# Plain float32 products for the first batch, and float16 weight parts made once behind it

## The chip, the cores and the metric

The kernel runs on one core of one Trainium2 chip. The time is device microseconds of one execution. TensorE (PE in the profile; PEld is its weight load) does the matrix products, VectorE (DVE) and ScalarE (ACT) the elementwise work, GpSimd (POOL) very little, and SyncE (SP) issues the DMAs.

## The reference

Attention over 8 batches, 8 heads, 576 positions, 64 columns a head, and then a gated layer over the 512 columns of all heads:

```python
scores = where(0 <= i - j < 128, q @ k.T / 8 - slope[h] * |i - j|, -1e9)
x = softmax(scores) @ v                      # heads side by side: 576 x 512
h = maximum(x @ w_in, 0)                     # w_in 512 x 1024
u, v = h[:, :512], h[:, 512:]
v_n = (v - mean(v)) / sqrt(var(v) + 1e-6)    # over its 512 columns
v_s = w_spatial @ v_n + b_spatial[:, None]   # w_spatial 576 x 576
out = (u * v_s) @ w_out                      # w_out 512 x 512
```

The weights `w_in` and `w_out` come as 64-bit floats, all else as float32.

## The kernel before

A batch has four pairs of heads and one gated stage. A pair's two heads stand on the two halves of the partitions. For batches 1 to 7 a pair takes: load (`L`), the score products (`P`, line 791, plain float32 on 64x64 quarters of the array), softmax on VectorE and ScalarE (`C`, lines 805 to 851), a DMA that turns the probabilities, the split of the values (`V`) and the product with them (`A`, line 937), whose result is a tile of x, `xt`. Batch 0 does the same in small tiles of 128 positions, so that work starts early: `t` (line 686), `m`, `n` (lines 728 and 743).

The gated stage has units, each an accumulation in one PSUM bank of the two named `m`:

- `v`, five of them: 128 positions by 512 columns of x @ w_in (line 1026; the last, of 64 positions, lines 1048 and 1054), then relu, layer norm, and the split of v_n into two float16 parts;
- `u`, eight: 128 columns by 288 positions (line 1083), then relu;
- `s`, eight: the product over positions with w_spatial in float16 parts (line 1104), then the gate (line 1112) and a split of the gated tile `gs` (lines 413 and 1118);
- `o`, eight: the output product (line 1130), copied out and stored.

Every product of two float32 operands is made of three matmuls: high by high, high by low, low by high (`PASS`). Batches 0 and 1 take w_in and x as two parts of type float32r (one pass each); batches 2 to 7 (`HALVES = 2`) take float16 parts. The output product is in float32r parts in all batches. `split_w64` turns 64-bit weights into float32 with some bit operations on VectorE (lines 432 to 451) and then makes the two float32r parts: a rounding copy (line 413) and a difference (line 456). For batch 2, `H`, `J`, `K` find a power of two (`win_limit`, `win_scale`) and make float16 parts of w_in from the float32r parts (`win_halves`, lines 508, 515, 519). The values of batch 1 get a power of two each by an own chain with a DMA (lines 878 to 898), those of later batches one for each batch.

`Plan` sets the order. Each operation has an engine, a weight in ns and a due time. `record` adds operations in the order of the table `OPENING` (then of `usual`), which fixes what waits for what and which buffer each takes. `Plan.forward` then lets each engine take the ready operation with the smallest due time, and `backward` sets the due times anew; an operation that either of VectorE and ScalarE can do goes to the one free first. Each engine executes in the emitted order. Where the plan has TensorE idle for over 400 ns between 9 and 95 us, it puts in matmuls of ones that compute nothing (`filler`, line 339); 64 of the same kind stand at the start (line 396).

Of the kernel before, what the change touches and what calls it, by code (L numbers as in the profile page):

```python
# [209 lines left out]
def attn_gmlp_kernel(ctx, tc, qk, v, w_in, w_spT, b_sp, w_out, outT):  # L210
# [85 lines left out]
    win = {(h, c): plan.buf(work, f"win{h}{c}", 1, [P, 2, DH], F32R) for h in range(2) for c in range(NC_)}  # L296
    win16 = {}
    wend = fixed([P, 2, DH], F16, "wend")
    wlim = fixed([P, 2, NC_], F32, "wlim")
# [120 lines left out]
    def split_w64(src, dst, tmp, hi, lo, due):  # L420
# [46 lines left out]
    def win_weights(half, c, due, st):  # L467
        w = win[half, c]
        split_w64((st, DH), (w, ()), plan.buf(work, "gs", 5, [P, DH], F32), lambda: w()[:, 0, :], lambda: w()[:, 1, :], due)

    def power(out, least, low):
        nc.vector.tensor_reduce(least, wide()[:, 1, :], AX.X, ALU.max)
# [16 lines left out]
    def win_limit(half, c, due):  # L489
        if half and c == NC_ - 1:  # L490
            w = wend
        else:
            w = plan.buf(work, *(("vraw", 3) if half else (f"win1{c}", 1)), [P, 2, DH], F16)
        win16[half, c] = w

        def f():
            nc.scalar.activation(w()[:, 0, :].bitcast(BF16), win[half, c]()[:, 0, :].bitcast(F32), AF.Abs, accum_out=wlim()[:, half, c:c + 1])
        plan.add("ACT", act(DH, 2), due, f, [(win[half, c], (0,))], [(w, 0), (wlim, (half, c))])

    def win_scale(half, due):  # L500
        sc = lambda a, z: wsc()[:, half, a:z]
        spread(lambda: sc(2, 3), lambda: wlim()[:, half, :], due, [(wlim, (half, c)) for c in range(NC_)], [(wsc, (half, 2))])
        plan.add("DVE", 1025, due + 2, lambda: power(sc(0, 2), sc(3, 4), 2.0 ** -12), [(wide, 1), (pow2, 0)], [(wsc, half)])

    def win_halves(half, c, due):
        w, x, sc = win16[half, c], win[half, c], lambda: wsc()[:, half, 0:1]
        old = lambda k: x()[:, k, :].bitcast(F32)
        plan.either([("ACT", act(DH, 1), lambda: nc.scalar.activation(w()[:, 0, :], old(0), AF.Copy, scale=sc())),
                     ("DVE", dve(DH, True) + 50, lambda: nc.vector.tensor_scalar(w()[:, 0, :], old(0), sc(), None, ALU.mult))],
                    due, [(x, (0,)), (wsc, half)], [(w, 0)])  # L510

        t = plan.buf(work, "vt", 2, [P, DH], F32)

        def f():
            nc.vector.scalar_tensor_tensor(t(), old(0), sc(), w()[:, 0, :], ALU.mult, ALU.subtract)
        plan.add("DVE", dve(DH) + 50, due + 1, f, [(x, (0,)), (wsc, half), (w, 0)], [(t, 0)])

        def f():
            nc.vector.scalar_tensor_tensor(w()[:, 1, :], old(1), sc(), t(), ALU.mult, ALU.add)
        plan.add("DVE", dve(DH) + 50, due + 2, f, [(t, 0), (x, (1,)), (wsc, half)], [(w, 1)])  # L520
# [16 lines left out]
    def wsp_load(c, due):  # L537
# [6 lines left out]
        def f():  # L544
            nc.scalar.activation(wsp()[:, c, 1, :].bitcast(BF16), st(), AF.Abs, accum_out=rows()[:, c:c + 1])
        plan.add("ACT", act(S, 2), due, f, [(st, 0)], [(wsp, (c, 1)), (rows, c)])

    def rest_load(due):
# [10 lines left out]
        def f():  # L559
            nc.scalar.activation(r1().bitcast(BF16), rs(), AF.Abs, accum_out=rows()[:, NQ - 1:NQ])  # L560
        plan.add("ACT", act(S, 2), due, f, [(rs, 0)], [(r1, 0), (rows, NQ - 1)])

        def f():
            nc.scalar.activation(r2()[b1, :].bitcast(BF16), bt()[b1, :], AF.Abs, accum_out=rows()[b1, NQ:NQ + 1])
        plan.add("ACT", act(S, 2), due, f, [(bt, 0), (r2, 2), (rows, "z")], [(r2, 1), (rows, NQ)])

    def weights_scale(due):

        def f():
            nc.vector.tensor_reduce(rows()[:, LEAST:LEAST + 1], rows()[:, :NQ + 1], AX.X, ALU.max)  # L570
            nc.vector.tensor_copy(wide()[:, 0, :], rows()[:, LEAST:LEAST + 1].to_broadcast([P, P]))
        plan.add("DVE", 320, due, f, [(rows, c) for c in range(NQ + 1)], [(wide, 0)])

        def f():
            nc.sync.dma_start_transpose(out=wide()[:, 1, :], in_=wide()[:, 0, :])
# [9 lines left out]
        plan.add("DVE", 700, due + 2, f, [(wide, 1)], [(rows, "s")])  # L585
# [33 lines left out]
    def tail(xt, due):  # L619

        copy(R, lambda: (xt()[:, S:S + R], xt()[:, 2 * S:2 * S + R]), due, xcols(xt, 1, (NQ - 1) * P, S), [(xt, 2)], fast=True)

    def load(b, p, due, pieces, values, raw=None, vr=None):
# [3 lines left out]
        if values:  # L627
            vr = vr or plan.buf(work, "vraw", 3, [P, NQ, P], F32)
# [642 lines left out]
```

## Time and profile before

| what | us |
|---|---|
| median of 3 runs | 551.82 |
| lowest and highest of them | 549.66, 552.36 |
| the profiled execution | 549.37 |
| its span, from the first to the last instruction | 547.6 |
| TensorE matmul busy | 529.6 (97%) |
| VectorE, ScalarE busy | 449.8 (82%), 417.4 (76%) |

A share of the span is a mean over very different stretches. Matmul records overlap (the next begins before the one before has ended), so a busy TensorE may still do little; what a unit costs is read from one unit's start to the next's.

### The profile page before, as it was taken

Reading aid. Unit: us, or ns where it says so; the run is one execution under the profiler, and the core shown is the slowest. Engines: PE = TensorE matmul, PEld = TensorE weight load, DVE = VectorE, ACT = ScalarE, POOL = GpSimd, SP = SyncE. Lnnn points to the kernel's source line nnn. Section 1 sums busy time; section 2 is a strip of 40 time slices with the busy share of each in tenths; the row PEclk is TensorE's granted clock in tenths of the full one; section 3 lists DMA queues with packets and bytes.
Section 4 is the critical chain, followed back from the end, with each engine's and each line's share of the span. In section 5 each row is a group of like instructions: output and inputs, shape, how many; then the busy total and the mean of one; then the engine's idle time right before and its main releaser. Section 6 shows DMA issues by size and latency. Waiting matters only on the chain.

```text
span 547.6 us, 16355 instructions
## 1 busy us (share of the span) xinstructions
PE 529.6 (97%) x6240; PEld 420.9 (77%) x6240; DVE 449.8 (82%) x1685; ACT 417.4 (76%) x1331; POOL 30.4 (6%) x75
## 2 busy tenths in 40 slices
PE   8889998989999999999999999999999999999997
PEld 5546886878889668896789858896689858884787
DVE  6999999989999996979998889978998798525440
ACT  7999999989889686969898768766976777424322
POOL 0000010000100020000200010000100010001000
PEclk9999999999999999999999999999999999999999
DMA  7974563977486833697567775866186524410002
GB/s 227 381 262 147 123 171 84 210 130 173 70 188 156 233 67 91 140 238 191 115 137 176 184 137 86 178 160 118 45 125 168 98 60 68 89 47 22 1 1 88
DMA packets 128468, 73.75 MB, mean 135 GB/s; under 512 B 106755, under 2 KB 119043, under 8 KB 128389
## 3 DMA queue, kind: packets, MB, share of 16 engines
q1 hardware_dynamic: 128388, 72.70, 56.3%
q8 instruction: 49, 0.80, 0.6%
q14 instruction: 31, 0.25, 0.1%
HBM read 37.13 MB, written 9.44 MB: 85 GB/s over the span
## 4 chain that ended last, share of the span: by engine, by line
PE 74%; ACT 9%; DVE 9%; DMA 4%; issue 2%; SPq 1%; POOL 1%; POOLq 0%; ACTq 0%; DVEq 0%
PE m L1104 18%; PE m L1130 16%; PE m L1083 15%; PE m L1026 12%; PE s L791 6%; PE x L937 5%; DVE pq L845 2%; DMA vraw<-in_v_dram 2%; ACT prob L811 1%; DMA qkraw<-in_qk_dram 1%; PE m L1048 1%; DVE prob L805 1%; DMA vl<-vl 1%; ACT pq L840 1%; SPq L632 1%
## 5 line engine op out<-in xcount | busy, mean ns | idle before, releaser
L1104 PE MATMUL m<-wsp,vn 128*128 128x288 f16 x768 | 110.9, 286 | 0.5 <-DVE vn L1037 0.5
L811 ACT ACTIVATE prob<-prob,stat 128x192 f32<-128x192 f32 (+2 forms) x252 | 107.4, 432 | 1.6 <-DVE stat L805 1.3
L1083 PE MATMUL m<-xt,win 128*128 128x288 f16 (+1 forms) x768 | 102.9, 289 | 2.4 <-DVE u L1112 1.6
L1130 PE MATMUL m<-gs,wout 128*128 128x288 f32 x732 | 103.0, 298 | 2.1 <-ACT o L413 1.8
L1130 PEld LDWEIGHTS m<-gs,wout 128*128 128x128 f32 x732 | 98.0, 188 | 3.9 <-ACT o L413 2.0
L840 ACT ACTIVATE pq<-prob,stat 128x192 f16<-128x192 f32 (+2 forms) x252 | 89.9, 428 | 6.6 <-issue 3.4
L845 DVE SCALAR_TENSOR_TENSOR pq<-prob,stat,pq 128x192 f16<-128x192 f32 (+2 forms) x252 | 87.4, 389 | 2.1 <-ACT pq L840 1.9
L1104 PEld LDWEIGHTS <-vn 128*128 128x128 f16 x768 | 73.9, 98 | 19.9 <-DVE vn L1037 0.8
L805 DVE CUSTOM_DVE_ANT_0 prob<-s,tabs 128x192 f32<-128x192 f32 (+2 forms) x252 | 71.0, 329 | 4.5 <-PE s L791 4.4
L1083 PEld LDWEIGHTS <-win 128*128 128x128 f16 x576 | 55.8, 98 | 15.7 <-issue 0.4
L1026 PEld LDWEIGHTS <-xt 128*128 128x128 f16 x288 | 27.0, 98 | 33.1 <-issue 2.1
L1026 PE MATMUL m<-vraw,xt 128*128 128x512 f16 x216 | 50.7, 380 | 0.0
L811 ACT ACTIVATION_READ_ACCUMULATOR prob<-prob,stat 128x1 f32 x252 | 48.9, 194 | 0.0
L413 ACT CAST gs<-u 128x288 fp32r<-128x288 f32 x50 | 21.4, 429 | 36.0 <-DVE u L1112 35.8
L791 PE MATMUL s<-qkraw 64*64 64x192 f32 (+1 forms) x1008 | 43.5, 310 | 0.0
L937 PEld LDWEIGHTS <-vh 64*64 64x64 f16 x1232 | 34.8, 106 | 9.4 <-issue 6.6
L937 PE MATMUL x<-pt,vh 64*64 64x192 f16 (+2 forms) x1232 | 39.7, 224 | 1.7 <-POOL am L946 1.7
L1112 DVE SCALAR_TENSOR_TENSOR u<-m,vsc,u 128x288 f32<-128x288 f32 x48 | 24.7, 514 | 20.0 <-PE m L1104 19.5
L996 POOL TENSOR_TENSOR st<-st,nhalf 128x1 f32<-128x1 f32 (+1 forms) x40 | 26.4, 660 | 208.8 <-DVE st L992 196.2
L987 DVE BATCH_NORM_STATS2 st<-vt 128x6 f32<-128x512 f32 (+1 forms) x40 | 27.4, 687 | 12.6 <-ACT vt L417 12.6
L791 PEld LDWEIGHTS s<-qkraw 64*64 64x64 f32 x1008 | 36.5, 133 | 0.8 <-DVE stat L834 0.2
L1118 DVE TENSOR_TENSOR gs<-u,gs 128x288 fp32r<-128x288 f32 x61 | 27.2, 453 | 9.0 <-ACT gs L413 8.6
(203 smaller groups left out, 837.2 us busy)
## 6 DMA issues: line engine op xcount, KB each, us to landing
qkraw<-in_qk_dram SPq DMA_DIRECT2D x28, 576.0 KB, 4.7
out_dram<-o SPq DMA_DIRECT2D x64, 144.0 KB, 1.9
wraw<-in_v_dram SPq DMA_DIRECT2D x12, 320.0 KB, 3.2
win<-in_v_dram SPq DMA_DIRECT2D x12, 320.0 KB, 3.5
wout<-in_w_in_dram SPq DMA_DIRECT2D x4, 512.0 KB, 6.2
vn<-in_w_in_dram SPq DMA_DIRECT2D x4, 512.0 KB, 7.9
wout<-in_w_out_dram SPq DMA_DIRECT2D x4, 512.0 KB, 3.6
vraw<-in_v_dram SPq DMA_DIRECT2D x4, 320.0 KB, 4.4
```

What stands on the lines that cost most here:

```text
L791: nc.tensor.matmul(flat(bank)[rows, c0:c0 + n], raw()[j * D:(j + 1) * D, 0, i * D:(i + 1) * D], raw()[j * D:(j + 1) * D, 1, (i + 1) * D - ...
L805: nc.vector.tensor_tensor_reduce(pt(), flat(bank)[:, c0:c0 + n], tabs()[:, 2 * p + odd, W - n:], -0.125, 3e38, ALU.add, ALU.min, st()[:, N ...
L811: nc.scalar.activation(pt(), pt(), AF.Exp, bias=st()[:, NM, k:k + 1], scale=-1.0, accum_out=st()[:, SM, k:k + 1])
L840: nc.scalar.activation(pq()[:, qc:qc + n], prob()[:, pc:pc + n], AF.Copy, scale=st()[:, RC, k:k + 1])
L845: nc.vector.scalar_tensor_tensor(pq()[:, qc + PLANE:qc + PLANE + n], prob()[:, pc:pc + n], st()[:, RC, k:k + 1], pq()[:, qc:qc + n], ALU.m ...
L937: done.append(nc.tensor.matmul(xps[half]()[j * D:(j + 1) * D, x0:x0 + len(ks) * D], l()[rows, kb // 2, j * D:(j + 1) * D], ap, start=(half ...
L987: nc.vector.bn_stats(st()[:m, 0:6], vt()[:m])
L1026: nc.tensor.matmul(pt(), xs(xt[c], a, t * P, (t + 1) * P), w[1, c]()[:, k, :], start=(n == 0), stop=(n == 3 * NC_ - 1))
L1083: nc.tensor.matmul(pt()[:, :HS], w[0, c]()[:, k, d * P:(d + 1) * P], xs(xt[c], a, hf * HS, (hf + 1) * HS), start=(n == 0), stop=(n == 3 * ...
L1104: nc.tensor.matmul(pt()[:, :HS], l, r, start=(n == 0), stop=(n == len(ops) - 1))
L1118: nc.vector.tensor_tensor(gs()[:, 1, :], u(), gs()[:, 0, :].bitcast(F32), ALU.subtract)
L1130: nc.tensor.matmul(pt()[:, :HS], wout[d]()[:, w, e * P:(e + 1) * P], gs[d]()[:, a, :], start=(n == 0), stop=(n == 3 * ND - 1))
```

## The change

Batch 0 has x as one float32 tile and w_in and w_out as one float32 tile (`exact`, twelve buffers `wx`). Its `v`, `u` and `o` units take four plain float32 matmuls in place of twelve of one pass. Batches 1 to 7 all take float16 parts: `win_halves` makes those of w_in from the exact weights before batch 1, `wout_limit`, `wout_scale`, `wout_halves` (`h`, `q`, `Z`) three float16 tiles of w_out (high, low, high / 1024) before the `o` units of batch 1. The limits of w_in and w_spatial are summed by TensorE (a matmul of ones with absolute values, lines 500 and 584 to 586) and not by an accumulating ScalarE instruction and a DMA. Values of batch 1 are scaled like those of later batches. The float32r parts, the differences that made them, and the copy of x's tail go. `OPENING` is another permutation, with `h`, `q`, `Z`, and with `D`, `G`, `E`, `O` of batch 1 added. x tiles are kept by the pair's number.

```diff
-        copy(n, lambda: (hi(), x()), due + 4, [X], [HI], fast=True)
-
-        def f():
-            nc.vector.tensor_tensor(lo(), x(), hi().bitcast(F32), ALU.subtract)
-        plan.add("DVE", dve(n), due + 5, f, [X, HI], [LO])
...
     def win_weights(half, c, due, st):
+        x = exact[half, c] = plan.buf(work, "wx", WX, [P, DH], F32)
+        bits64((st, DH), x, due)
...
+                nc.tensor.matmul(pt(), sums()[:, 1, :], win[half, c]()[:, 0, :].bitcast(BF16), start=(c == 0), stop=(c == NC_ - 1))
+        plan.add("PE", pe16(*[DH] * NC_), due, f, [(win[half, c], 0) for c in range(NC_)] + [(sums, 0)], [(pt, 0)])
...
+    def parted16(w, x, sc, n, due, reads):
+        plan.either([("ACT", act(n, 1), lambda: nc.scalar.activation(w()[:, 0, :], x(), AF.Copy, scale=sc())),
+                     ("DVE", dve(n, True) + 50, lambda: nc.vector.tensor_scalar(w()[:, 0, :], x(), sc(), None, ALU.mult))],
+                    due, reads, [(w, 0)])
+
+        def f():
+            nc.vector.scalar_tensor_tensor(w()[:, 1, :], x(), sc(), w()[:, 0, :], ALU.mult, ALU.subtract)
+        plan.add("DVE", dve(n) + 50, due + 1, f, reads + [(w, 0)], [(w, 1)])
+
+    def wout_halves(c, due):
+        w = wout[c] = plan.buf(work, f"wout{c}", 1, [P, 3, DM], F16)
+        parted16(w, exact["o", c], lambda: olim()[:, 4:5], DM, due, [(exact["o", c], 0), (olim, 4)])
...
-        def f():
-            nc.vector.tensor_tensor(xt()[:, S + R + qs.start:S + R + qs.stop], xp()[:, :m], xt()[:, qs].bitcast(F32), ALU.subtract)
-        plan.add("DVE", dve(m), due + 1100, f, [(xp, 0)] + xh, xl)
-        if t == NQ - 1:
-            tail(xt, due + 1200)
...
+            if b == 0:
+                def f():
+                    for c in range(NC_):
+                        nc.tensor.matmul(pt(), xt[c]()[:, t * P:(t + 1) * P], exact[1, c](), start=(c == 0), stop=(c == NC_ - 1))
+                plan.add("PE", pe(*[4 * DH] * NC_), due, f, [k for x in xt for k in xcols(x, 0, t * P, (t + 1) * P)] + [(exact[1, c], 0) for c in range(NC_)], [(pt, 0)])
...
+            if b == 0:
+                def f():
+                    for d in range(ND):
+                        nc.tensor.matmul(pt()[:, :HS], exact["o", d]()[:, e * P:(e + 1) * P], gs[d](), start=(d == 0), stop=(d == ND - 1))
...
+                        for a, w in ((0, 0), (0, 1), (1, 2)):
+                            nc.tensor.matmul(pt()[:, :HS], wout[d]()[:, w, e * P:(e + 1) * P], gs[d]()[:, a, :],
+                                             start=(n == 0), stop=(n == 3 * ND - 1))
```

The order on TensorE where batch 1's gated stage begins, before. `qkraw` are the queries and keys of a later pair (line 791), `win` the float32r parts of w_in, `xt` x; each row's `x3` are the three passes of one 128-row piece:

```order
L791 MATMUL s_67<-qkraw 64x128 x2
L1026 MATMUL m<-win_375,xt 128x512 x3
L1026 MATMUL m<-win_623,xt 128x512 x3
L1026 MATMUL m<-win_572,xt 128x512 x3
L1026 MATMUL m<-win_514,xt 128x512 x3
L1083 MATMUL m<-xt,win_353 128x288 x3
```

The same place now. Line 1090 is the output product of batch 0 from the exact weights `wx`, line 1003 the 64-position `v` unit of batch 1 from float16 parts:

```order
L1090 MATMUL m<-gs,wx 128x288 x12
L1003 LDWEIGHTS xt
L1003 MATMUL m<-win_82,xt 64x512
L1003 LDWEIGHTS xt
L1003 MATMUL m<-win_82,xt 64x512
```

In both programs all `v`, `u`, `s` units of batch 0, seven of its eight `o` units and four products with values (`A`) stand ahead of this place; six score products (108 instructions of line 791) stood ahead of it and five (90 of line 794) do now. No filler is left in the program.

The order on TensorE where batch 0's `v` units begin, before (`ident` turns probabilities, line 728; line 743 is the product with values):

```order
L743 MATMUL x_70<-pq,vraw 64x128 x4
L728 MATMUL m<-ident,prob 128x128 x2
L1026 MATMUL m<-win_375,xt 128x512 x3
L1026 MATMUL m<-win_623,xt 128x512 x3
L1026 MATMUL m<-win_572,xt 128x512 x3
L1026 MATMUL m<-win_514,xt 128x512 x3
L728 MATMUL m<-ident,pt 128x128 x2
```

And now (lines 738 and 753 are the former 728 and 743):

```order
L738 MATMUL m<-ident,prob 128x128 x2
L753 MATMUL x_70<-pq,vraw 64x128 x4
L738 MATMUL m<-ident,pt 128x128 x2
L967 MATMUL m<-wx,xt 128x512 x8
L738 MATMUL m<-ident,prob 128x128 x4
L753 MATMUL x_71<-pq,vraw 64x64 x4
```

Two `v` units of four matmuls each stand in a row where one unit of twelve stood; the small products for the last positions of batch 0 come behind them.

## Rows read from the trace of the kernel before

**Rows 1.** The page: busy us and share of the span by engine.
```profile
PE 529.6 (97%) x6240; PEld 420.9 (77%) x6240; DVE 449.8 (82%) x1685; ACT 417.4 (76%) x1331; POOL 30.4 (6%) x75
```

**Rows 2.** Busy time by stretch; TensorE's granted clock (1.00 full) follows POOL.
```profile
core 0: us, PE busy (x) PEld busy (x) DVE busy (x) ACT busy (x) POOL busy (x), PEclk, DMA share, GB/s
0.00:123.75 123.75, 110.68 (x1308) 86.50 (x1308) 115.32 (x464) 115.36 (x376) 4.67 (x16) 1.00 0.69 192
123.75:185.15 61.40, 60.75 (x748) 53.46 (x745) 59.82 (x218) 50.86 (x163) 3.90 (x9) 1.00 0.68 157
185.15:547.60 362.45, 358.14 (x4190) 280.91 (x4188) 274.67 (x1006) 251.20 (x794) 21.82 (x50) 1.00 0.51 111
20.00:30.00 10.00, 7.33 (x77) 4.55 (x71) 9.32 (x34) 9.46 (x34) 0.00 (x0) 1.00 1.05 376
313.00:374.00 61.00, 61.00 (x774) 48.07 (x773) 52.49 (x200) 46.77 (x154) 3.44 (x9) 1.00 0.66 137
```

**Rows 3.** TensorE by line: warm-up and filler matmuls (count, busy us, mean ns).
```profile
L396 PE MATMUL x<-ones 128*128 128x256 bf16 x64 | 10.4, 318 | 1.0 <-DVE halves L357 1.0
...
L339 PE MATMUL s<-ones 128*128 128x128 bf16 x64 | 5.3, 220 | 0.0
```

**Rows 4.** The chain of waits, 0 to 135 us: start us, length us, what.
```profile
86.90 0.60 DVE wout L456
...
110.50 6.02 DMA vl<-vl
```

**Rows 5.** The chain of the whole span: units in later batches.
```profile
169.27 6.54 PE m L1130 x48
175.81 5.18 PE m L1104 x42
...
256.14 5.29 PE m L1026 x24
...
266.67 7.35 PE m L1083 x60
```

**Rows 6.** The page's costliest groups: weight loads of two kinds, and two casts.
```profile
L1130 PEld LDWEIGHTS m<-gs,wout 128*128 128x128 f32 x732 | 98.0, 188 | 3.9 <-ACT o L413 2.0
...
L1104 PEld LDWEIGHTS <-vn 128*128 128x128 f16 x768 | 73.9, 98 | 19.9 <-DVE vn L1037 0.8
...
L413 ACT CAST gs<-u 128x288 fp32r<-128x288 f32 x50 | 21.4, 429 | 36.0 <-DVE u L1112 35.8
...
L1118 DVE TENSOR_TENSOR gs<-u,gs 128x288 fp32r<-128x288 f32 x61 | 27.2, 453 | 9.0 <-ACT gs L413 8.6
```

**Rows 7.** The chain around 70 us: units of batch 0 and a score product.
```profile
68.38 2.12 PE m L1054 x8
...
72.37 1.46 PE s L791 x32
73.83 2.94 PE m L1026 x12
```

**Rows 8.** TensorE in order of time: start us, length us, instruction, count.
```profile
61.81 6.51 PE L1083 MATMUL m<-xt,win 128*128 128x288 f32 x48
```

**Rows 9.** VectorE by line.
```profile
L456 DVE TENSOR_TENSOR win<-gs,win 128x512 fp32r<-128x512 f32 x8 | 5.4, 684 | 0.0
...
L751 DVE TENSOR_TENSOR xt<-x,xt 128x128 fp32r<-128x128 f32 x16 | 4.5, 279 | 0.6 <-ACT xt L413 0.6
...
L515 DVE SCALAR_TENSOR_TENSOR vt<-win,wsc,win 128x512 f32<-128x512 f32 x4 | 3.0, 746 | 0.0
```

**Rows 10.** ScalarE by line.
```profile
L413 ACT CAST win<-gs 128x512 fp32r<-128x512 f32 x7 | 4.6, 650 | 0.0
...
L508 ACT ACTIVATE win<-win,wsc 128x512 f16<-128x512 f32 x4 | 2.8, 725 | 0.0
L497 ACT ACTIVATE win<-win 128x512 bf16<-128x512 f32 x4 | 2.5, 628 | 0.9 <-DVE vraw L519 0.9
```

**Rows 11.** What TensorE waited for before 200 us: us in total, times, longest.
```profile
PE m L1130 <- ACT o L413: 1.8, 1, 1.8
```

More of the change, by code (lines that the diff above doesn't have):

```diff
@@ L295, in attn_gmlp_kernel @@
     tabs = fixed([P, H, W], BF16, "tabs")
[L296 to L299, printed above, removed]
+    win = {(h, c): fixed([P, 2, DH], F16, f"win{h}{c}") for h in range(2) for c in range(NC_)}
+    exact = {}
     wsc = fixed([P, 2, 4], F32, "wsc")
+    olim = fixed([P, 8], F32, "olim")
     vsc = [fixed([P, 16], F32, f"vsc{k}") for k in range(3)]
@@ L308, in attn_gmlp_kernel @@
     wide = fixed([P, 2, P], BF16, "wide")
+    sums = fixed([P, 2, P], BF16, "sums")
     FIRSTS = (NB + 1) // 2
@@ L467, in win_weights, with power @@
     def win_weights(half, c, due, st):
[L468 to L472, printed above, removed]
+        x = exact[half, c] = plan.buf(work, "wx", WX, [P, DH], F32)
+        bits64((st, DH), x, due)
+    def power(out, least, low, limits):
+        nc.vector.tensor_reduce(least, limits, AX.X, ALU.max)
         nc.vector.tensor_scalar(least, least, low, 2.0 ** 110, ALU.max, ALU.min)
@@ L500, in win_scale @@
+        plan.add("ACT", act(DH), due, f, [(x, 0)], [(w, 0)])
     def win_scale(half, due):
         sc = lambda a, z: wsc()[:, half, a:z]
-        spread(lambda: sc(2, 3), lambda: wlim()[:, half, :], due, [(wlim, (half, c)) for c in range(NC_)], [(wsc, (half, 2))])
-        plan.add("DVE", 1025, due + 2, lambda: power(sc(0, 2), sc(3, 4), 2.0 ** -12), [(wide, 1), (pow2, 0)], [(wsc, half)])
-    def win_halves(half, c, due):
[L506 to L512, printed above, removed]
-        def f():
[L515 to L520, printed above, removed]
@@ L567, in weights_scale @@
+        plan.add("ACT", act(S), due, f, [(bt, 0), (r2, 2)], [(r2, 1)])
     def weights_scale(due):
+        pts = [plan.buf(ps, "m", 2, [P, 512], F32) for _ in range(2)]
         def f():
[L570 to L575, printed above, removed]
@@ L576, in weights_scale @@
-        plan.add("SP", 300, due + 1, f, [(wide, 0)], [(wide, 1)], lag=1500)
+            for hf, pt in enumerate(pts):
+                cs = slice(hf * HS, (hf + 1) * HS)
+                for c in range(NQ - 1):
+                    nc.tensor.matmul(pt()[:, :HS], sums()[:, 0, :], wsp()[:, c, 1, cs].bitcast(BF16), start=(c == 0), stop=False)
+                nc.tensor.matmul(pt()[:, :HS], sums()[0:R, 0, :], r1()[0:R, cs].bitcast(BF16), start=False, stop=False)
+                nc.tensor.matmul(pt()[:, :HS], sums()[b1, 1, :], r2()[b1, cs].bitcast(BF16), start=False, stop=True)
@@ L578, in f @@
+        plan.add("PE", pe16(*[HS] * 12) + 60, due, f, [(wsp, (c, 1)) for c in range(NQ - 1)] + [(r1, 0), (r2, 1), (sums, 0)], [(pt, 0) for pt in pts])
         def f():
             least, sc = rows()[:, LEAST:LEAST + 1], scale()
-            nc.vector.tensor_reduce(least, wide()[:, 1, :], AX.X, ALU.max)
+            for k, pt in enumerate(pts):
+                nc.vector.tensor_reduce(rows()[:, k:k + 1], pt()[:, :HS], AX.X, ALU.max)
+            nc.vector.tensor_tensor(least, rows()[:, 0:1], rows()[:, 1:2], ALU.max)
@@ L584, in f @@
             nc.vector.tensor_scalar(sc.bitcast(I32), sc.bitcast(I32), BITS, None, ALU.bitwise_xor)
-        plan.add("DVE", 700, due + 2, f, [(wide, 1)], [(rows, "s")])
+        plan.add("DVE", 800 + 2 * dve(HS), due + 2, f, [(pt, 0) for pt in pts], [(rows, "s")])
     def wsp_weights(c, due):
@@ L616, in rest_weights, with load @@
         plan.add("DVE", dve(S) + 50, due, f, [(bt, 0), (r2, 1), (rows, "s")], [(r2, 1)])
-    def tail(xt, due):
-        copy(R, lambda: (xt()[:, S:S + R], xt()[:, 2 * S:2 * S + R]), due, xcols(xt, 1, (NQ - 1) * P, S), [(xt, 2)], fast=True)
-    def load(b, p, due, pieces, values, raw=None, vr=None):
+    def load(b, p, due, pieces, raw=None):
         raw = raw or plan.buf(work, "qkraw", 3, [P, 2, S], F32)
-        if values:
-            vr = vr or plan.buf(work, "vraw", 3, [P, NQ, P], F32)
         src = qk[b, 2 * p:2 * p + 2].rearrange("h d a s -> (h d) a s")
@@ L1151, in attn_gmlp_kernel @@
     w_u = [win_load(0, c, UDUES[c], f"wout{c}", 1) for c in range(NC_)]
-    outs[0] = [plan.buf(work, "xt", 6, [P, 2 * S + R], F32R) for _ in range(NP)]
+    outs[0] = {p: plan.buf(work, "xt", XT, [P, S], F32) for p in range(NP)}
     def record(kind, b, p):
```

316 lines of the change are left out of this document (152 added, 164 removed), and 16 rows, old and new, of the table OPENING.

## The prediction

> **What bounds the kernel now.** I read the page first: TensorE's matmuls are busy 97% of the span, VectorE 82%, ScalarE 76% [rows 1]. Such shares hide stages, so the table by stretch comes next, cut at two units: the first gated unit of batch 1 at 123.75 us, the first of batch 2 at 185.15 us [rows 2]. Ahead of the first cut VectorE and ScalarE are each busy 115.3 of 123.75 us, 93%. TensorE is busy 110.7, but 10.4 of that are warm-up matmuls and 5.3 fillers [rows 3], so with its 13.1 idle us it has some 28 us to spare there. Behind the cut TensorE is idle for 0.65 of 61.4 us and 4.3 of 362.4 us, and a steady batch (313 to 374 us) leaves VectorE 8.5 us free while TensorE has no idle time. The chain of waits agrees: from 80 to 134 us it runs over VectorE and ScalarE work and one DMA of 6.02 us that spreads a maximum of batch 1's values [rows 4], later over units of TensorE that follow each other [rows 5]. So there are two stages with two limits: an opening of 124 us that VectorE and ScalarE share, and 424 us of TensorE. I work out each by itself.
>
> **TensorE, behind the cut.** One pass over 288 columns costs 7.35 / 60 = 0.1225 us in float16 (line 1083) and 6.54 / 48 = 0.136 us in the output product's float32r (line 1130) [rows 5]. The float32r weight load takes 188 ns, the float16 one 98 [rows 6]: longer than the pass itself, so it is no longer hidden.
>
> - Output units of batches 1 to 7: 56 units of 12 passes, 1.635 us each now, 1.47 in float16: 56 x 0.165 = -9.2 us.
> - Batch 1's four large `v` units: 2.94 us in float32r [rows 7], 5.29 / 2 = 2.65 in float16 [rows 5]: -1.2.
> - Its 64-position unit: 2.12 us for eight passes [rows 7]; in float16 twelve half-width matmuls lie two side by side, six times 5.29 / 24 = 0.22: 1.3 us, so -0.8.
> - Its eight `u` units: four took from 61.81 to 68.38 us [rows 7, 8], 1.64 each; in float16 1.47: -1.4.
> - The order moves one score product of 1.46 us [rows 7] from ahead of the cut to behind it, and one output unit of batch 0 there becomes plain float32 (+0.3, below): +1.8.
>
> Sum: -10.8 us. TensorE ends each of these stretches, so I count it in full. What could take it back: an output copy with a scale held in memory and a difference that multiplies cost VectorE and ScalarE more, by my estimate 0.1 us each, 16 instructions a batch, 1.6 us. The 8.5 free us of a steady batch cover it [rows 2]. Between 124 and 185 us VectorE is at 59.8 of 61.4; there the splitting of w_in for batch 2 goes (eight tiles of three instructions of about 0.73 us [rows 9, 10]) and that of w_out comes (four tiles of three): less than before, cost nothing. Without that cover the 12 added instructions would cost up to 8 us.
>
> **TensorE, ahead of the cut.** No plain float32 matmul of 128 x 128 by 512 is in the trace. The nearest row is a score product: 18 plain float32 matmuls, 3072 columns on quarters of the array, four side by side. At the 0.43 ns a column of the float16 row (0.22 / 512) one pass would take 3072 x 0.43 / 4 = 0.33 us; it took 1.46 [rows 7], 4.4 passes with the gaps at the ends. So I take four passes, 0.88 us for 512 columns and 0.49 for 288; 4.4 passes is the upper end, and the lower is no loss at all (three float32r passes cost as much). A unit of four such matmuls is 3.5 us (`v`, and the 64-position one) or 1.96 (`u`, `o`). Against float32r: `v` 4 x 0.58 = 2.3, the 64-position unit 3.5 - 2.12 = 1.4, `u` 8 x 0.32 = 2.6, seven `o` units 2.3. The sums of absolute weights add twelve passes of 288 columns and eight of 512, 1.5 + 1.8 = 3.2 us. The score product that moved takes 1.5 off. Sum: +10.3 us (0 to +15), against 28 us to spare. In a stage that VectorE and ScalarE limit I count it at nothing; if that cover fails, all of it shows.
>
> By the Trainium skill (TensorE: Matmul & The Clock Gate, Weight-path perf modes) fast weight loads are for weights that are not float32, which speaks against the plain products. The trace bears the rule out for float32r, 188 ns against 98 [rows 6]. For the plain ones it would add time only where a load is longer than the work that it stands behind, and a two-pass half of 288 columns is 0.245 us, so by the rule too the sum stays.
>
> **VectorE and ScalarE, ahead of the cut.** What goes, by records: twelve rounding copies of weights at 0.65 us [rows 10] and twelve differences at 0.68 [rows 9], 16.0; twenty differences of x at 0.28 [rows 9], 5.6; batch 0's sixteen casts and differences of the gated tile at about 0.44 [rows 6], 7.0; about 6 us of small instructions (the tails of x, the scale chain of batch 1's values), an estimate from their number, 35, at 0.15 to 0.25. Together 35. What comes, since batch 1 needs float16 w_in: eight high parts at 0.73 and eight low ones at 0.75 [rows 9, 10], 11.8; seven absolute values more than stood there, at 0.63 [rows 10], 4.4; and about 5 for scales read from PSUM and batch 1's own. Together 21. Records overlap at their ends: a difference of 0.68 takes 0.60 in the chain [rows 4, 9], so 0.88 of the net: -12 of the 230.7 us that both are busy. Shared evenly, the 123.75 us become 117.3, -6.4. But the differences that go are VectorE's and the copies that go are mostly ScalarE's, and the low parts that come are VectorE's: if VectorE alone paces the stage, next to nothing comes off. I take -3. The lower end is -12 (shared evenly, and the 6.02 us DMA goes from the chain with nothing late in its place), the upper end +10 (TensorE's addition in full). What is late next, where the DMA went, is VectorE itself.
>
> DMAs move the same bytes; in SP's queue two pieces of w_spatial now stand ahead of the last pieces of batch 0's keys and two pieces of w_in behind them, which I count at nothing, as both lie in a stretch with DMA at its limit (1.05 of 1 between 20 and 30 us [rows 2]).
>
> **Sum.** 549.4 - 10.8 - 3 = 535.6 us against the profiled execution. That one lies 2.4 us under the median of the runs shown, 551.8, from which the same terms give 538.0. I predict 538.
>
> **Rivals.**
> 1. The opening grows by all that TensorE gets. The plain units are blocks of 2 to 3.5 us (two of them in a row at the first one) in an in-order queue, and the small products that feed VectorE and ScalarE wait behind them. For it: those two have no slack to catch up with. Against: TensorE's 28 us to spare, and the room that the fillers had. +10.3 - 10.8: 551.3, no change.
> 2. Slower: the same place, but a plain matmul costs the score product's 4.4 passes and each of them shows. 84 plain matmuls are 47 us at four passes; a tenth more is 4.7, so the opening grows by 15: 556. It turns slower from 13.6 us of growth on (10.8 and the 2.8 that a measurement needs). Against it: the 28 us to spare.
> 3. The clock falls. The changed program has no filler, and 64 stood before. The granted clock is 1.00, the higher level, in every stretch, also where TensorE was idle 2.7 of 10 us, fillers counted as work [rows 2], and the longest wait before 200 us, 1.8 us for an output copy, did not lower it [rows 11]. If it halved between 20 and 60 us, work of some 29 us (7.3 of each 10 [rows 2]) would take 58 and outrun the spare time by a few us: 544. The Trainium skill (TensorE: Matmul & The Clock Gate, HAM oscillation) says that the clock drops to half after idle time; no run here shows a fall.
> 4. The opening gains in full: -10.8 - 10: 531.
>
> **Chances.** Forecast (534 to 543) 0.64; rival 1 0.13; rival 2 0.05; rival 3 0.05; rival 4 0.13. What a measurement can tell from no change is about 0.5%, 2.8 us: under 549.0 is faster. The forecast, 3 and 4 are faster, 0.82; rival 1 is within, 0.12, with 0.01 of it and rival 2 slower, 0.06. The range 530 to 548 leaves out rivals 1 and 2 and little more; the forecast's own range is 534 to 543.
>
> **What would show it.** Output units of batches 1 to 7 at 1.47 us, pass to pass 0.1225; a steady batch shorter by 1.3 us; plain `v` units at 3.5 us and `u`, `o` units at 1.96; the first gated unit of batch 1 at 117 to 124 us with VectorE over 90% busy ahead of it; a granted clock of 1.00 throughout. I am wrong if that unit starts after 128 us, if idle time of TensorE appears behind it, or if VectorE ends steady batches.

## The result

The changed kernel takes 537.16 us (median of four runs, 536.89 to 537.46) against 551.43 (549.66 to 552.36): a ratio of 0.9745, 95% interval 0.9719 to 0.9771. The prediction was 538 (530 to 548). The profiled execution took 537.46 us with a span of 535.7, against 549.37 and 547.6 before.

First the page's busy line of the changed kernel, which answers to [rows 1]:

```profile
PE 526.4 (98%) x6118; PEld 381.3 (71%) x6120; DVE 443.9 (83%) x1654; ACT 404.3 (75%) x1278; POOL 28.4 (5%) x75
```

Then its busy time by stretch, in the columns of [rows 2]. The first gated unit of batch 1 now starts at 121.59 us, the first `v` of batch 2 at 183.40:

```profile
0.00:121.59 121.59, 116.81 (x1150) 78.14 (x1152) 115.18 (x448) 108.91 (x346) 4.75 (x16) 1.00 0.73 207
121.59:183.40 61.81, 61.81 (x806) 45.66 (x806) 55.47 (x220) 51.95 (x174) 3.69 (x9) 1.00 0.69 158
183.40:535.70 352.30, 347.79 (x4164) 257.51 (x4164) 273.25 (x987) 243.48 (x759) 19.93 (x50) 1.00 0.49 110
```

Three things are to be seen here. The opening is 2.2 us shorter (123.75 before), all that lies behind it 9.7 us (423.85 to 414.11). Ahead of the cut VectorE did as much as before, ScalarE 6.5 us less and TensorE 6.1 more, though 5.3 us of fillers went: it is now busy 116.8 of 121.6 us. Cut at 60 us, hardly anything is left over behind that point, 1.4 us on TensorE and 1.0 on VectorE; the last line is the same stretch of the kernel before, where TensorE had 5.1 us idle:

```profile
0.00:60.00 60.00, 56.58 (x534) 35.11 (x535) 54.59 (x241) 56.39 (x187) 2.50 (x9) 1.00 0.81 266
60.00:121.59 61.59, 60.24 (x618) 43.03 (x618) 60.59 (x209) 52.52 (x160) 2.25 (x7) 1.00 0.65 151
...
60.00:123.75 63.75, 58.65 (x758) 51.31 (x756) 60.62 (x227) 60.04 (x187) 2.74 (x8) 1.00 0.69 153
```

The chain of waits behind the cut (start, length, what), as [rows 5]; line 1098 is the output product in float16, 1058 the spatial product, 1037 `u` and 974 `v`:

```profile
121.66 1.42 PE m L1003 x12
123.08 1.58 PE m L1037 x12
...
165.25 5.99 PE m L1098 x48
171.24 5.14 PE m L1058 x42
...
222.50 5.88 PE m L1098 x48
...
315.01 5.29 PE m L974 x24
```

A unit of the output product takes 5.88 / 4 = 1.47 to 5.99 / 4 = 1.50 us where it took 6.54 / 4. Its weight load is 98 ns now, as the page shows, where it was 188 [rows 6]:

```profile
L1098 PE MATMUL m<-gs,wout 128*128 128x288 f16 x636 | 81.1, 286 | 0.0
...
L1098 PEld LDWEIGHTS <-wout 128*128 128x128 f16 x672 | 64.8, 98 | 16.7
```

That the load sets the price is not shown, and the `v` units speak against it. With 512 columns a pass is longer than a load of 188 ns, and float32r costs more there too: before, a unit of batch 1 took 126.61 - 123.75 = 2.86 us from its start to the next line's, 0.238 us a pass; now three units take 7.78 us, 0.216 a pass. First the lines of before, then those of now:

```profile
123.75 3.02 PE L1026 MATMUL m<-win,xt 128*128 128x512 f32 x12
126.61 0.69 PE L1083 MATMUL m<-xt,win 128*128 128x288 f32 x4
...
126.05 7.94 PE L974 MATMUL m<-win,xt 128*128 128x512 f16 x36
133.83 1.63 PE L1037 MATMUL m<-xt,win 128*128 128x288 f16 x12
```

So a float32r pass is some 10% longer at either width, 0.136 against 0.123 us and 0.238 against 0.216. Why it is longer stays open.

Batch 0's plain float32 units on TensorE in order of time: `v` is line 967, `u` 1029, the output product 1090. Two `v` units take 47.87 - 41.00 = 6.87 us to the next instruction, 3.4 each; one from 56.12 to 59.66, 3.5. Three output units from 115.58 to 121.59 take 2.0 each:

```profile
41.00 7.03 PE L967 MATMUL m<-wx,xt 128*128 128x512 f32 x16
...
56.12 3.70 PE L967 MATMUL m<-wx,xt 128*128 128x512 f32 x8
59.66 2.10 PE L1029 MATMUL m<-xt,wx 128*128 128x288 f32 x8
...
115.58 6.09 PE L1090 MATMUL m<-gs,wx 128*128 128x288 f32 x24
121.59 1.49 PE L1003 MATMUL m<-win,xt 128*64 128x512 f16 x12
```

### The profile page after: what moved, and what is told of

Same layout as the page of the kernel before. It is cut to its first block, busy times and chain, and to the rows that moved or that the text cites. A ratio compares the mean times of both kernels' runs of the same rounds, so it can differ in the third digit from the quotient of the medians.

```text
span 535.7 us, 15979 instructions
## 1 busy us (share of the span) xinstructions
PE 526.4 (98%) x6118; PEld 381.3 (71%) x6120; DVE 443.9 (83%) x1654; ACT 404.3 (75%) x1278; POOL 28.4 (5%) x75
## 4 chain that ended last, share of the span: by engine, by line
PE 81%; DVE 10%; DMA 4%; issue 3%; SPq 1%; POOL 0%; ACT 0%; POOLq 0%; ACTq 0%; DVEq 0%
PE m L1058 21%; PE m L1098 16%; PE m L1037 15%; PE m L974 12%; PE s L794 6%; PE x L896 6%; PE m L1090 3%; DMA wout<-in_w_in_dram 3%; PE m L1003 2%; DVE pq L848 1%; DVE prob L808 1%; DMA qkraw<-in_qk_dram 1%; SPq L639 1%; DVE st L932 1%; PE m L1029 1%
## 5 line engine op out<-in xcount | busy, mean ns | idle before, releaser
L1037 PE MATMUL m<-xt,win 128*128 128x288 f16 x672 | 88.0, 286 | 0.1
L1098 PE MATMUL m<-gs,wout 128*128 128x288 f16 x636 | 81.1, 286 | 0.0
L1037 PEld LDWEIGHTS <-win 128*128 128x128 f16 x672 | 65.2, 98 | 18.8 <-issue 0.8
L1098 PEld LDWEIGHTS <-wout 128*128 128x128 f16 x672 | 64.8, 98 | 16.7
L974 PE MATMUL m<-win,xt 128*128 128x512 f16 x336 | 75.7, 379 | 0.7 <-ACT vt L416 0.7
L974 PEld LDWEIGHTS <-xt 128*128 128x128 f16 x336 | 32.0, 98 | 39.3 <-issue 3.5
L1074 ACT ACTIVATE gs<-u 128x288 f16<-128x288 f32 x44 | 19.4, 441 | 36.2 <-DVE u L1071 36.1
L896 PEld LDWEIGHTS <-vh 64*64 64x64 f16 x1232 | 34.7, 106 | 10.3 <-issue 7.9
L1071 DVE SCALAR_TENSOR_TENSOR u<-m,u 128x288 f32<-128x288 f32 x56 | 25.5, 455 | 19.6 <-PE m L1058 19.0
L932 DVE BATCH_NORM_STATS2 st<-vt 128x6 f32<-128x512 f32 (+1 forms) x40 | 27.5, 687 | 11.0 <-ACT vt L416 10.7
L941 POOL TENSOR_TENSOR st<-st,nhalf 128x1 f32<-128x1 f32 (+1 forms) x40 | 24.4, 611 | 205.5 <-DVE st L937 186.1
L917 ACT ACTIVATE xt<-x 128x320 f16<-128x320 f32 (+1 forms) x56 | 19.7, 403 | 19.0 <-PE x L896 19.0
```

The lines of the kernel that those rows point to most:

```text
L896: done.append(nc.tensor.matmul(xps[half]()[j * D:(j + 1) * D, x0:x0 + len(ks) * D], l()[rows, kb // 2, j * D:(j + 1) * D], ap, start=(half ...
L932: nc.vector.bn_stats(st()[:m, 0:6], vt()[:m])
L974: nc.tensor.matmul(pt(), xt[c]()[:, a, t * P:(t + 1) * P], w[1, c]()[:, k, :], start=(n == 0), stop=(n == 3 * NC_ - 1))
L1037: nc.tensor.matmul(pt()[:, :HS], w[0, c]()[:, k, d * P:(d + 1) * P], xt[c]()[:, a, hf * HS:(hf + 1) * HS], start=(n == 0), stop=(n == 3 * ...
L1071: nc.vector.scalar_tensor_tensor(u(), pt()[:, :HS], GATE * FINE, u(), ALU.mult, ALU.mult)
L1098: nc.tensor.matmul(pt()[:, :HS], wout[d]()[:, w, e * P:(e + 1) * P], gs[d]()[:, a, :], start=(n == 0), stop=(n == 3 * ND - 1))
```

## The experiments

Each ratio is against the kernel before as timed in the same round; its median lay between 550.39 and 551.43 us in the rounds, so a difference of about 1 us between two medians of this table is not resolved. "Opening" is the start of batch 1's first gated unit in the profiled run.

| kernel | median us | ratio (95%) | opening |
|---|---|---|---|
| before | 551.43 | 1 | 123.75 |
| changed | 537.16 | 0.9745 (0.9719 to 0.9771) | 121.59 |
| 1 changed, output product in float32r | 545.54 | 0.9916 (0.9889 to 0.9942) | 120.95 |
| 2 before, output product in float16 | 543.32 | 0.9849 (0.9830 to 0.9868) | 124.79 |
| 3 before, order of the changed | 553.00 | 1.0044 (1.0027 to 1.0061) | 131.31 |
| 4 changed, order of before | 542.21 | 0.9859 (0.9825 to 0.9892) | 126.15 |
| 5 less TensorE work in the opening | 536.14 | 0.9748 (0.9720 to 0.9777) | 120.01 |
| 6 more of it | 548.89 | 0.9978 (0.9957 to 0.9998) | 132.31 |
| 7 more VectorE work | 544.51 | 0.9896 (0.9871 to 0.9922) | 128.58 |
| 8 less of it | 538.27 | 0.9773 (0.9751 to 0.9794) | 122.53 |
| 9 more ScalarE work | 542.81 | 0.9861 (0.9841 to 0.9882) | 126.97 |
| 10 less TensorE and VectorE work | 535.54 | 0.9709 (0.9685 to 0.9734) | 120.36 |
| 11 as 10, with fillers | 534.82 | 0.9716 (0.9699 to 0.9733) | 120.71 |
| 12 ScalarE work put on GpSimd | 541.21 | 0.9807 (0.9784 to 0.9830) | 125.79 |

**1, the output product alone put back.**

```diff
-            w = wout[c] = plan.buf(work, f"wout{c}", 1, [P, 3, DM], F16)
+            w = wout[c] = plan.buf(work, f"wout{c}", 1, [P, 2, DM], F32R)
...
-                        for a, w in ((0, 0), (0, 1), (1, 2)):
+                        for a, w in PASS:
```

> The changed kernel, with the output product of batches 1 to 7 put back into float32r (both operands split into float32r parts as before the change); order, plain products of batch 0 and all else as changed. Theory (behind the cut TensorE ends every stretch, and the output product's passes are most of the gain): 56 units go from 1.497 back to about 1.635 us, +7.7 us, so 545 us and 0.988 of the kernel before; a steady batch longer by 1.1 us. Rival (the gain is the new order's, or VectorE's): no more than +1 us, 538.

Measured: 545.54, +8.4, as the theory has it. Its opening is no longer than the changed kernel's, so all of it lies behind the cut; from each matmul's start to the next one's the 56 units take 91.2 us there, 82.7 in the changed kernel. Its chain (line 1103 is the product) and the page's weight load:

```profile
164.61 6.57 PE m L1103 x48
```

```profile
L1103 PEld LDWEIGHTS m<-gs,wout 128*128 128x128 f32 x636 | 85.3, 188 | 0.7
```

**2, the same part done alone.**

```diff
-        w = wout[c] = plan.buf(work, f"wout{c}", 1, [P, 2, DM], F32R)
+        w = wout[c] = plan.buf(work, f"wout{c}", 1, [P, 2, DM], F16)
...
-            gs = gss[hf, d] = plan.buf(work, *(("qkraw", 3) if b == B - 1 and k > 4 else ("gs", 5)), [P, 2, HS], F32R)
+            gs = gss[hf, d] = plan.buf(work, *(("qkraw", 3) if b == B - 1 and k > 4 else ("gs", 5)), [P, 2, HS], F16)
```

> One part of the change alone: the kernel before, with both operands of its output product split into float16 parts (unscaled) in place of float32r ones, by the same instructions in the same order; the rest as before. Theory (TensorE ends every stretch behind the opening, and the output product's passes are most of the gain): the 56 units of batches 1 to 7 fall from 1.635 to about 1.5 us, -7.7, and batch 0's eight are hidden in the opening or add another -1: 0.984 to 0.987 of the kernel before, 542.5. Rival (other parts give it): 0.995 or more.

Measured: 0.9849, 8.3 us of the change's 14.1. Runs 1 and 2 agree: the output product's passes are some 60% of the gain, in either program.

**3 and 4, the order.** The sequence of weight tiles, raw attention and absolute sums in `OPENING` exchanged, all else left at its place. The table's beginning in run 3:

```diff
-        "t02 t03 t00 t11 t10 t01 X00 w00 m00 n00
...
+        "w00 t02 X00 t01 t11 X01 t12 a00 t03 t00 m00 n00
...
```

> The kernel before, with the tiles of weights, the raw attention of batch 0 and the sums of absolute weights in the order of the changed kernel (the same steps in the changed kernel's sequence, at the places that such steps hold); arithmetic as before. Theory (the arithmetic gives the gain): 548 to 556 us, no gain. Rival (the order gives it): 545 or less.

> The changed kernel, with the tiles of weights, the raw attention of batch 0 and the sums of absolute weights in the sequence that the kernel before has for them (at the places that such steps hold in the changed kernel). Theory (the new order serves the opening alone; what lies behind the first gated unit of batch 1 keeps its 9.7 us): 540 to 550 us, all of the difference ahead of that unit. Rival (the order is worth nothing here): 537 within 1.

Measured: the old arithmetic gains nothing from the new sequence (+0.4%); its opening is longer, too (by 7.6 us in the profiled execution, the slowest of ten). The new arithmetic under the old sequence loses 5.0 us, its opening 4.6: it ends at 126.15 us, later than the 123.75 of before, while what lies behind keeps its gain (span 540.4 - 126.15 = 414.2, as 414.1). So neither the old arithmetic under the new sequence nor the new one under the old sequence shortens the opening. Both kernels are hybrids of two orders: they show what these sequences are worth, not what the best one would give.

**5 and 6, TensorE's work in the opening.** Run 5 leaves a matmul out in all units of batch 0; run 6 has `(0, 1, 1, 2, 3)` there:

```diff
-                    for c in range(NC_):
+                    for c in (0, 2, 3):
```

> The changed kernel, with one of the four plain float32 matmuls left out of every unit of batch 0 (so a quarter of batch 0's products isn't computed): 5 x 0.88 + 16 x 0.49 = 12.2 us less TensorE work, 11.7 of it ahead of the first gated unit of batch 1. Theory A (as predicted: VectorE and ScalarE pace the opening, TensorE's added work is hidden there): -1 to 0 us, 536.5. Theory B (TensorE has become the end of the opening from about 65 us on): -5 to -9 us, 530; the first gated unit of batch 1 starts at 113 to 117 us in place of 121.6.

> The changed kernel, with one of the four plain float32 matmuls of every unit of batch 0 done twice (so that share of batch 0's products counts double): 12.2 us more TensorE work, 11.7 of it ahead of the first gated unit of batch 1. Theory A as the prediction has it (TensorE's work is hidden there, 28 us to spare before the change): 0 to +2 us, 539. Theory C (A still held for the change itself, but has used the spare time up: TensorE is idle 4.8 us of the opening's 121.6 and 1.4 us behind 60 us): +8 to +11 us, 547.

Measured: 11.7 us off gave 1.0 (no difference by the ratios), 11.7 us on cost 11.7, a little over theory C's range. TensorE's work was hidden, and the cover ended just there. Busy time by stretch from 60 us to the first gated unit of batch 1, run 5 and then run 6 (columns as above):

```profile
60.00:120.01 60.01, 53.31 (x586) 36.72 (x586) 59.16 (x204) 51.25 (x159) 2.11 (x7) 1.00 0.63 148
```

```profile
60.00:132.31 72.31, 71.21 (x659) 50.12 (x658) 63.64 (x215) 54.41 (x166) 2.09 (x7) 1.00 0.59 132
```

In run 5 TensorE has 6.7 us to spare and VectorE 0.9: VectorE ends it. In run 6 it is TensorE, with 1.1 us idle, and VectorE has 8.7. The clock fell in run 5 (below), so it is not TensorE's work alone that differs; among its four executions the time does not follow the clock, though (537.43 us at a mean of 1.000, 535.34 to 536.15 at 0.997 to 0.999).

**7 and 8, VectorE's work.** Run 7 adds a line behind the last step of `bits64`; run 8 leaves that last step out in its place:

```diff
             nc.vector.scalar_tensor_tensor(xi(), low(), 29, xi(), ALU.logical_shift_right, ALU.bitwise_or)
+            nc.vector.tensor_tensor(scratch(), x(), x(), ALU.subtract)
```

> The changed kernel, with one more VectorE difference of 128 x 512 float32 (0.68 us) behind the last step of each of the twelve weight tiles, into a buffer nobody reads: as many as the change took from VectorE there, 8.2 us, eight tiles ahead of about 50 us and four behind it. Theory A (VectorE paces the opening): +6 to +8 us, 544. Theory B (TensorE ends it from about 65 us on, VectorE paces only what lies ahead of that): +2 to +5 us, 540.5. Rival (VectorE has room): 0.

> The changed kernel, without the last VectorE step on each of the twelve weight tiles (the lowest three bits of the float32 weights stay zero): 12 x 0.69 = 8.2 us less VectorE work by records. If VectorE alone paced the opening and nothing stood behind it: -7 us, 530, as the +7.4 us for twelve added ones. Theory C (TensorE's work stands close behind VectorE's): the tiles that come ahead of 50 us count and the rest meets TensorE, -3 to -5 us, 533; the first gated unit of batch 1 at 116.5 to 118.5 us. Rival (TensorE already ends it): -1 to 0 us.

Measured: +7.4 us for twelve more, +1.1 for twelve fewer. So theory A, which foresaw run 5 and 7, falls at run 8, and so does C's -3 to -5; the rival, -1 to 0, comes nearest. With VectorE relieved, TensorE ends the second half of the opening, as run 8's stretch shows (TensorE idle 1.2 us, VectorE 2.8):

```profile
60.00:122.53 62.53, 61.32 (x623) 43.51 (x622) 59.77 (x210) 53.70 (x166) 2.21 (x7) 1.00 0.65 148
```

**9, ScalarE's work**, for the tiles of w_in, and likewise for those of w_spatial:

```diff
             nc.scalar.activation(w()[:, 0, :].bitcast(BF16), x(), AF.Abs)
+            nc.scalar.copy(scratch(), x())
```

> The changed kernel, with twelve more ScalarE copies of 128 x 512 float32 into a buffer nobody reads, one behind the absolute values of each of four tiles of w_spatial and eight of w_in: 12 x 0.65 = 7.8 us more ScalarE work, where the change took off 6.5. Theory (VectorE paces the opening, ScalarE has 12.7 us idle in it): 0 to +3 us, 538.5. Rival (the two share the pace, as the prediction's even share had it): +4 to +7 us, 543.

Measured: +5.7 us; the rival holds. Eight of the twelve copies (5.0 us) stand ahead of 53 us, four behind 75. The first `u` unit of batch 0 starts at 58.97 us and not at 53.60: the whole loss in the opening, 5.4 us, is made by then, and the last four copies cost nothing. That fits ScalarE's idle time, 12.7 us in the changed opening, of which 9.1 lie behind 60 us. Ahead of that `u` unit TensorE waits for ScalarE, and then its clock falls (a mean of 0.83 from 50 to 60 us): the 36 matmuls of a score product take 2.66 us in place of 1.53. So the clock may have a part in the 5.7 us; how large a one is not shown. First the changed kernel, then run 9:

```profile
51.54 1.53 PE L794 MATMUL s<-qkraw 64*64 64x192 f32 x36
...
53.60 2.21 PE L1029 MATMUL m<-xt,wx 128*128 128x288 f32 x8
```

```profile
52.02 0.44 PE L741 MATMUL m<-ident,pt 128*128 128x128 f32 x2 [1.94 <-ACT vt L417]
53.53 0.66 PE L741 MATMUL m<-ident,pt 128*128 128x128 f32 x4 [1.07 <-ACT pq L413]
...
55.79 2.66 PE L797 MATMUL s<-qkraw 64*64 64x192 f32 x36
...
58.97 2.21 PE L1032 MATMUL m<-xt,wx 128*128 128x288 f32 x8
```

**10 and 11, two engines relieved at once** (the edits of runs 5 and 8; run 11 adds fillers, shown here):

```diff
                         nc.tensor.matmul(pt(), xt[c]()[:, t * P:(t + 1) * P], exact[1, c](), start=(c == 0), stop=(c == NC_ - 1))
+                    begun.append(t)
+                    if len(begun) == 2:
+                        filler(28)
```

> The changed kernel with both of the reductions that gave nothing alone: one of four plain matmuls left out of each unit of batch 0 (TensorE -11.7 us ahead of batch 1's first gated unit; alone -1.0) and no last VectorE step on the twelve weight tiles (VectorE -8.2; alone +1.1). Theory D (the opening is balanced: VectorE and TensorE are both full behind 60 us, so that either one alone frees nothing): together -4 to -7 us, 532. Theory E (ScalarE, full from 10 to 60 us, sets the first half whatever the other two do): -1 to -3 us, 535.

> The kernel with both reductions (a plain matmul of four left out of batch 0's units, and no last VectorE step on twelve weight tiles; -1.6 us against the changed kernel), with 28 filler matmuls of 128 columns behind the second v unit of batch 0, where TensorE there stood idle for 1.9 us at 46.6 us and the granted clock was then 0.73 between 50 and 60 us. Theory (the fall of the clock took part of what the two reductions free): clock 1.00 in 50 to 60 us, -2 to -4 us against that kernel, 532.5. Rival (VectorE, full from 60 us on, sets the end whatever the clock does): within 0.7 us of it, 535.5.

Measured: -1.6 us (0.9709 against 0.9745), theory E's range; the fillers gave nothing more (0.9716). VectorE is nearly full from 60 us on: only four of the twelve tiles lie there. Run 10 from 60 us to the first gated unit:

```profile
60.00:120.36 60.36, 54.80 (x589) 37.28 (x589) 58.64 (x206) 52.30 (x165) 2.11 (x7) 1.00 0.63 152
```

Run 11's profile doesn't settle what the clock took. The fillers restored it between 50 and 60 us (0.73 to 1.00), but another wait of TensorE came earlier and it fell there, 0.88 between 40 and 50:

```profile
40.00:50.00 10.00, 10.00 (x83) 5.94 (x77) 7.30 (x27) 8.06 (x21) 0.92 (x1) 0.88 0.35 117
50.00:60.00 10.00, 10.00 (x112) 6.90 (x110) 8.76 (x41) 9.92 (x34) 0.56 (x1) 1.00 0.70 247
```

The single executions say more. In run 10 the two with a mean clock of 0.999 and 1.000 took 534.87 and 534.42 us, the two with 0.994 took 536.22 and 536.53. In run 11 the three at 1.000 took 534.63 to 534.82, those at 0.999 and 0.997 535.88 and 536.94. So a lower clock goes with 1 to 2 us here, and without it both reductions together give 2.3 to 2.7 us, still in theory E's range.

**12, ScalarE's passes over weights on GpSimd.**

```diff
-            nc.scalar.activation(w()[:, 0, :].bitcast(BF16), x(), AF.Abs)
+            nc.gpsimd.tensor_scalar(w()[:, 0, :].bitcast(BF16), x(), 0.0, None, ALU.max)
```

> The changed kernel, with the twelve passes over weight tiles that ScalarE makes for the sums of absolute weights (0.62 to 0.69 us each, 7.4 us) put on GpSimd, which is busy 5% of the span (it takes the positive weights alone). Theory D (balanced, one engine alone frees nothing): -1 to +1 us, 537. Theory E (ScalarE sets the first 60 us): -3 to -6 us, 532.5.

Measured: +4.0 us, foreseen by neither. GpSimd's pass is some 2.6 times as long as ScalarE's 0.62 and 0.69 us, so that the weights probably come later, and TensorE's clock fell too (0.73 from 34 to 40 us). So the run says nothing on theory E:

```profile
L491 POOL TENSOR_SCALAR win<-wx 128x512 bf16<-128x512 f32 x8 | 12.8, 1609 | 2.6 <-DVE wx L449 2.6
L555 POOL TENSOR_SCALAR wsp<-wraw 128x576 bf16<-128x576 f32 x4 | 7.3, 1839 | 17.6 <-DMA wraw<-in_w_spT_dram 17.6
```

```profile
30.00:34.00 4.00, 2.32 (x23) 1.37 (x24) 3.97 (x19) 3.49 (x12) 1.49 (x1) 0.98 0.86 240
34.00:40.00 6.00, 6.00 (x41) 3.52 (x40) 4.96 (x17) 5.13 (x17) 0.00 (x0) 0.73 0.88 344
```

## Why the prediction was right, and what in it was not

**Behind the cut: right, a little too large.** -9.7 us measured, -10.8 forecast, all of it TensorE's. Added up from each matmul's start to the next one's, in both traces behind the cut:

| term | forecast | measured |
|---|---|---|
| output units, batches 1 to 7 | -9.2 | 56 x (1.632 - 1.477) = -8.7 |
| `v` units | -1.2 | 75.3 to 73.6: -1.8 |
| 64-position units | -0.8 | 10.4 to 10.7: +0.3 |
| `u` units | -1.4 | 85.0 to 83.5: -1.5 |
| score product moved | +1.5 | +1.5 |
| batch 0's one plain output unit | +0.3 | +0.3 |

The rest is +0.3 for the spatial products. The mis-sized terms are the output product, whose units now take 1.47 to 1.50 us and not all 1.47, and batch 1's 64-position unit. I priced that at batch 0's 2.12 us [rows 7]; batch 1's own took 1.85, and it takes 1.42 in float16, not 1.3. The +0.3 in that row is a wait: behind one such unit of a later batch TensorE now waits 0.7 us for ScalarE. A steady batch is 1.2 us shorter (`v` to `v` 59.8 us, from 61.0), for 1.3.

The prices came from rows and held. The reason that I gave for them, a weight load longer than the pass and so no longer hidden, does not fit: float32r costs some 10% more a pass at 512 columns too, where the load is shorter than the pass, and the plain matmuls, whose load is 186 to 190 ns, show no such loss.

**TensorE ahead of the cut: prices right, and the cover held, but with nothing over.** Plain `v` units take 3.4 to 3.5 us (3.5), `u` units 2.04 and `o` units 1.99 on the mean (1.96): four passes, not 4.4, so rival 2 falls. (Its 84 plain matmuls would be 49 us at my prices, not 47; nothing hangs on it.) TensorE's work there grew by 6.1 + 5.3 of fillers = 11.4 us (forecast 10.3). Counting it at nothing was right: in run 5, without 11.7 us of it, the time is the same within what can be measured. The step that failed is "28 us to spare". 10.4 of these were warm-up at the beginning, and 8.0 of the 13.1 idle us lay ahead of 60 us. What counts is the room behind 60 us: there TensorE had 5.1 us idle and 2.1 of fillers, and TensorE and VectorE now have 1.4 and 1.0 us left of 61.6. Run 6 shows rival 1's mechanism at once when more is added. Under the old sequence (run 4) the opening ends 2.4 us later than before, with TensorE idle 1.2 and VectorE 1.0 us behind 60 us; which of the two shows there was not separated. I counted the order of the opening at nothing; by run 4 it is worth some 5 us.

**VectorE and ScalarE: the sum was half of what I thought, the time about right.** Forecast -12 busy and -3 on the time; measured -0.1 on VectorE, -6.5 on ScalarE and -2.2. Added up by records the two did 11.7 us less (301.3 to 289.5; forecast 14), although the new order has six more softmax steps of VectorE (line 845, now 848) and five more of ScalarE (840, now 843) ahead of the cut, some 5 us that I did not count. Of the 11.7 us only 6.6 came off their busy time: the factor 0.88 for overlap was too large. I gave as the reason for -3 that VectorE alone might pace the stage. It does so in one direction only: +8.2 us of its work cost 7.4 (run 7), -8.2 gave nothing (run 8). The opening is close to balanced. VectorE, TensorE and ScalarE each make it longer when given more (runs 7, 6 and 9); TensorE or VectorE relieved alone does not shorten the time (5 and 8), and both together give 1.6 us (10). ScalarE was not relieved alone.

**The clock: rival 3 did not happen here, but its mechanism exists.** The granted clock is 1.00 in every stretch of the changed kernel, and no fillers were needed for it: TensorE's longest wait in the opening, once the warm-up has begun, is 0.6 us. In run 5, where these units are shorter, TensorE waited 1.5 and 0.6 us for ScalarE near 48 us, and then the clock was at its lower level, 0.50, from 50 to 53 us. TensorE's waits in that stretch (us, times, longest), and its busy time and clock by stretch:

```profile
PE m L738 <- ACT vt L416: 1.5, 1, 1.5
PE m L738 <- ACT pq L412: 0.6, 1, 0.6
```

```profile
46.00:50.00 4.00, 1.94 (x26) 1.23 (x24) 3.85 (x16) 4.00 (x13) 0.93 (x1) 0.98 0.28 82
50.00:53.00 3.00, 3.00 (x31) 2.41 (x34) 2.77 (x10) 3.00 (x13) 0.43 (x1) 0.50 0.53 182
53.00:60.00 7.00, 7.00 (x63) 4.32 (x56) 6.48 (x31) 6.80 (x25) 0.12 (x1) 0.98 0.87 272
```

The fall came to the kernel before, too, with its fillers, though not in its profiled execution. Over the rounds of the experiments 21 of its executions have a mean clock of 0.999 or 1.000 and a median of 549.9 us, 20 have 0.994 to 0.997 and a median of 551.4. The changed kernel's four are at 0.999 or 1.000.

The Trainium skill (TensorE: Matmul & The Clock Gate, HAM oscillation) says that waits between pieces of TensorE's work can throttle it again, with longer waits than these, for DMAs, as its case; this run agrees, 0.50 behind a stretch in which it was busy 1.94 of 4 us.

**The sum.** On the profiled executions it is -11.9 us where I had -13.8: 1.1 too much behind the cut and 0.8 too much ahead. The median came out nearer (537.16 for 538.0) because I carried over the 2.4 us by which the profiled run of before lay under its median; that of the changed kernel lies 0.3 over its own. Some 1.5 of those 2.4 us go with the clock (551.4 - 549.9), which the profiled run of before had in full and half of its executions had not. So two errors cancelled in part, and that the median came within 1 us of 538 is luck.

What stays open is what paces the first 60 us. The records point to ScalarE. Busy time from 10 to 60 us in the changed kernel, in run 8 and in run 9:

```profile
10.00:60.00 50.00, 47.95 (x457) 30.14 (x458) 47.74 (x193) 49.31 (x164) 1.48 (x2) 1.00 0.84 282
...
10.00:60.00 50.00, 47.37 (x456) 29.91 (x455) 43.03 (x183) 48.96 (x162) 1.49 (x2) 1.00 0.83 281
...
10.00:60.00 50.00, 44.01 (x436) 28.23 (x436) 43.96 (x169) 49.51 (x156) 1.49 (x2) 0.97 0.75 255
```

ScalarE is nearly full in all three. With 4.7 us less on VectorE (run 8) batch 0's first `u` unit starts 1.0 us later than in the changed kernel, not earlier; with eight differences more on VectorE ahead of it (5.5 us, run 7) it starts 2.3 us later, and with eight copies more on ScalarE (5.0 us, run 9) 5.4 us later. In run 8 the chain of waits goes over a DMA of weights until 33 us and then over ScalarE until 54. But no run took work away from ScalarE; run 12 was meant to and did not.

## What to carry to other kernels

Price each stretch by the engine that ends it. Here a float32r pass cost some 10% more than a float16 one, and the gain from leaving it was kept wherever TensorE is the end. Take such a price from rows, and test the reason for it on a second shape before passing it on. Spare time of an engine counts only in the stretch where the new work stands, not over the whole stage. Where several engines are nearly full, as in this opening, more work on any of them showed for the most part (11.7 of 11.7 us, 7.4 of 8.2, 5.7 of 7.8), and less on TensorE or VectorE alone did not show. Look at the granted clock of every execution, not only of the profiled one.

## What the runs showed of the hardware that I had not expected

- A plain float32 matmul of 512 columns takes 0.86 to 0.88 us and one of 288 columns 0.49 to 0.51 on the mean, as long as four float16 passes. Its weight load is 186 to 190 ns, as long as float32r's, and it adds nothing that shows: 4 x 0.1225 us is 0.49.
- A float32r pass takes 0.136 us at 288 columns and 0.238 at 512, where float16 takes 0.123 and 0.216.
- TensorE's clock fell to 0.50 after waits of 1.5 and 0.6 us close together (run 5), and to a mean of 0.73 from 34 to 40 us after a stretch of four in which it was busy 2.3 (run 12). In the profiled execution of the kernel before, the 1.8 us wait [rows 11], which stood alone, did not lower it.
- GpSimd took 1.61 us for a pass over 128 x 512 float32 (the larger of each value and 0), where ScalarE's (the absolute value) takes 0.62.
